# A lag-table generator with part of its arguments on ScalarE, its gate block interleaved, and its last output chunk in quarters

## The chip, the cores and the metric

One core of one Trainium2 chip. The metric is the device time of one execution in microseconds (us), median of the fast runs; a run more than 1.5% above the fastest of its kernel counts as slow and is left out. A profile is one execution; its span is about 1.7 us shorter than the time of the same execution. TensorE is called PE below, VectorE DVE, ScalarE ACT.

## The reference, cut to what matters

```python
x = A_u                                              # (1, 2048, 512)
g = sigmoid((x * gate_w).sum(-1, keepdims=True))     # the gate
a = ssm_conv(x)     # y = causal convolution of u with K, plus u*Dskip
b = moe(x)          # top 2 of 2048 tokens through one expert, scattered back onto x
return g * a + (1 - g) * b
# in ssm_conv:
P = exp(logdA[:, :, None] * l[None, None, :])        # complex, one row per lag l
K = einsum("dn,dnl,dn->dl", Cc, P, dB).real
```

The exponentials of all lags are built from two smaller tables: 32 coarse lags ("first table", groups of four, eight groups) and 21 fine lags ("second table", six groups, the last with one lag). The channels come in two halves, so each table is made twice.

## The kernel before

One group of four lags goes through these steps: `arg` (an angle in 16-bit turns, eight instructions), `sin` (one activation over the eight), `prod` (DVE multiplies with the decay that `exp` made on ACT; a *full product* below is the eight DVE instructions of a second-table group). `S.op` puts an instruction at the end of its engine's queue and derives its waits from the buffers it reads and writes; the program gives each engine one queue. A buffer is a name, not an address range: an instruction that writes `bYA[vb]` waits for everything that touched `bYA[vb]`, and also for the same engine's own earlier write to it.

```python
def lag_group(hh, lags, is_q, slot0, gi, stage):     # hh: half, is_q: second table, gi: buffer 0/1
    if stage == 'arg':
        for i, t in enumerate(lags):
            for cs in range(2):
                TS(ARG(...), B16(...), float(t), ALU.mult, [bB16], [bARG[gi]], s2=..., op1=ALU.add, eng=DVE)
    elif stage == 'exp':  ...   # one ACT instruction per lag
    elif stage == 'sin':
        ACTV(TRG(...gi...), ARG16(...gi...), ACTF.Sin, [bARG[gi]], [bTRG[gi]], ...)
    else: ...                   # prod: 2 DVE instructions (first table) or 8 (second table)
# ... [cut]
        def kgen_tables(hh):
            def block_(tab, is_q, ngr):
                lgp(0, 'arg'); lgp(1, 'arg')
                for g in range(ngr):
                    lgp(g, 'sin')
                    if not is_q and g == 5:
                        ...                       # the 21 exps of the second table
                    lgp(g, 'prod')
                    if g + 2 < ngr:
                        lgp(g + 2, 'arg')
                    if hh == 0: next(rm_gen, None)        # one step of routing and expert
                    else:       next(post_g[0], None)
            block_(LQ_T1, False, 8)
            block_(LQ_T2, True, 6)
            if hh == 0:
                ...                               # 32 exps of the second half's first table
```

Ahead of `kgen_tables(0)` stands the gate block: 64 transposes of the input on PE, eight evictions of them (copies of PE's results) on ACT into `XT`, four DVE multiplies, PE logits, sigmoid. After both tables of a half come 512 small strided matmuls (`kgen_mm`), then the spectral products. The last chunk's output is `xu_inv(3)`, `mix_a(3)`, `mix_p(3)`, `mix_o(3)`: eight evictions, one add, sixteen scalings on ACT, one add, one store, each over the whole chunk.

## Time and profile before

| | before |
|---|---|
| time, median of 16 runs | 394.99 us (392.92 to 397.87) |
| span of the profiled run | 396.1 us (that run: 397.87) |
| busy DVE / ACT / PE | 285.3 / 221.9 / 188.3 us |
| DVE busy in the gate block (24.2 to 43.6) | 5.5 of 19.4 us |

No engine is busy throughout. So what counts is not busy time but which wait ends last in each stage, and the working of the prediction reads it stage by stage from where one engine's instructions start. In a timeline row the columns are start, duration of the merged stretch, engine, line, operation, output and input with shapes, count, and in brackets the idle time just before and what ended it. L306 is the DVE helper with two tensor inputs, L309 a scaling, L310 the one that makes an argument, L314 a copy, L316 the activation helper; in the changed kernel L403 is an argument on ACT.

### The profile page before, as it was taken

To read this page: it belongs to the slowest core of one execution; us is meant where nothing else is said; L and a number is where in the kernel's file an instruction comes from. 1 tells how busy PE (TensorE), PEld (TensorE's weight loads), DVE (VectorE), ACT (ScalarE), POOL (GpSimd) and SP (SyncE) were. 2 spreads that over 40 slices of the span, in tenths; PEclk is the share of its full clock that TensorE was granted. 3 is DMA by queue.
4 is the path that set the end of the run, shared out by engine and by line. 5 is a ranking of instruction groups with operands and counts; after the bars stand their busy time and mean duration, and the time that the engine had idled before them with its cause. 6 is when DMAs were issued, how large, how long until landed. Compare 5 with 4: busy or idle time off the path is not lost.

```text
span 396.1 us, 8501 instructions
## 1 busy us (share of the span) xinstructions
PE 188.3 (48%) x3674; PEld 170.5 (43%) x3674; DVE 285.3 (72%) x537; ACT 221.9 (56%) x337; POOL 1.7 (0%) x6
## 2 busy tenths in 40 slices
PE   2503100331400073640179100779899999997900
PEld 2502000330100073530179100779879979885900
DVE  0842799525999995577149999999999099899331
ACT  3895453695313599768965225244553393571574
POOL 0000100000000000000000000000000000000000
PEclk9965555555855565585588855669978969968775
DMA  6998000031000000000000000000000000200222
GB/s 155 285 452 367 2 1 0 0 122 65 1 0 0 0 5 2 2 2 1 0 2 2 2 0 1 3 5 2 3 2 2 2 2 2 56 0 2 55 54 53
DMA packets 18213, 16.91 MB, mean 43 GB/s; under 512 B 12800, under 2 KB 17024, under 8 KB 18048
## 3 DMA queue, kind: packets, MB, share of 16 engines
q1 hardware_dynamic: 18176, 16.37, 12.5%
q8 instruction: 29, 0.48, 0.5%
q14 instruction: 8, 0.07, 0.1%
HBM read 14.27 MB, written 2.10 MB: 41 GB/s over the span
## 4 chain that ended last, share of the span: by engine, by line
DVE 37%; ACT 32%; PE 24%; issue 5%; SPq 1%; DMA 1%; ACTq 0%; DVEq 0%
DVE RT L306 23%; ACT RT L316 17%; DVE RT L310 11%; PE ps L729 9%; ACT RK L316 8%; PE ps L779 5%; ACT RT L793 3%; ACT L316 3%; PE ps L697 2%; PE ps L660 1%; PE ps L664 1%; PE ps L769 1%; PE ps L768 1%; ACT RS L316 1%; DMA RT<-in_A_C_im_dram 1%
## 5 line engine op out<-in xcount | busy, mean ns | idle before, releaser
L306 DVE TENSOR_TENSOR RT<-RT 128x1024 bf16<-128x1024 bf16 (+5 forms) x140 | 102.3, 743 | 34.8 <-ACT RT L316 17.6
L316 ACT ACTIVATE RT<-RT 128x2048 bf16<-128x2048 int16 (+1 forms) x28 | 50.9, 1817 | 59.3 <-DVE RT L310 59.3
L316 ACT ACTIVATE RT<-ps 128x512 bf16<-128x512 f32 (+3 forms) x79 | 52.3, 669 | 51.6 <-PE ps L729 22.8
L310 DVE TENSOR_SCALAR RT<-RS 128x256 int32<-128x256 f32 x212 | 70.3, 334 | 6.3
L306 DVE TENSOR_TENSOR RT<-RT,RK 128x4096 bf16<-128x4096 bf16 (+3 forms) x32 | 52.2, 1674 | 11.7 <-ACT RT L316 11.6
L660 PE MATMUL ps<-RT 128*32 128x24 bf16 x512 | 22.8, 290 | 65.0 <-DVE RT L306 65.0
L729 PE MATMUL ps<-RU,RC 128*128 128x128 bf16 x896 | 52.4, 222 | 2.6 <-ACT RK L316 2.6
L729 PEld LDWEIGHTS ps<-RU,RC 128*128 128x128 bf16 x896 | 51.8, 100 | 2.8 <-issue 2.8
L660 PEld LDWEIGHTS ps<-RT 128*32 128x32 bf16 x512 | 21.5, 173 | 66.3 <-DVE RT L306 65.3
L779 PE MATMUL ps<-RT,RC 128*128 128x128 bf16 x512 | 38.4, 252 | 3.0 <-DVE RT L306 3.0
L779 PEld LDWEIGHTS ps<-RT,RC 128*128 128x128 bf16 x512 | 37.7, 117 | 3.5 <-DVE RT L306 3.1
L697 PE MATMUL ps<-RS,RC 128*128 128x128 bf16 x288 | 21.5, 248 | 30.6 <-ACT RS L316 27.1
L697 PEld LDWEIGHTS ps<-RS,RC 128*128 128x128 bf16 x288 | 20.6, 114 | 31.4 <-ACT RS L316 27.6
L793 ACT ACTIVATE RT<-RT,RS 128x128 bf16<-128x128 bf16 x64 | 25.7, 401 | 14.2 <-DVE RT L306 12.2
L316 ACT ACTIVATE RT<-RS 128x256 bf16<-128x256 f32 x74 | 30.8, 416 | 3.5 <-DVE RS L306 1.2
L306 DVE TENSOR_TENSOR RT<-RK,RT 128x1024 bf16<-128x1024 bf16 x16 | 11.1, 691 | 26.5 <-ACT RT L316 26.3
L306 DVE TENSOR_TENSOR RT<-RT,RS 128x1024 bf16<-128x1024 bf16 (+1 forms) x48 | 27.7, 618 | 0.4
L316 ACT ACTIVATE RK<-ps 128x512 bf16<-128x512 f32 x32 | 19.1, 596 | 15.6 <-DVE RT L306 10.5
L664 PE MATMUL ps<-RT 128*32 128x24 bf16 x512 | 22.9, 290 | 4.2 <-issue 4.2
L664 PEld LDWEIGHTS ps<-RT 128*32 128x32 bf16 x512 | 21.9, 172 | 4.1 <-issue 4.1
L316 ACT ACTIVATE RK<-RS 128x256 bf16<-128x256 f32 x32 | 22.0, 687 | 1.0
L316 ACT ACT_TABLE_LOAD x12 | 15.4, 1283 | 0.9 <-PEq L869 0.7
(59 smaller groups left out, 149.6 us busy)
## 6 DMA issues: line engine op xcount, KB each, us to landing
RC<-c_mats SPq DMA_DIRECT2D x1, 5376.0 KB, 24.8
RU<-in_A_u_dram SPq DMA_DIRECT2D x4, 512.0 KB, 8.1
out_dram<-RT SPq DMA_DIRECT2D x4, 512.0 KB, 3.8
RK<-in_B_w_gate_dram SPq DMA_DIRECT2D x1, 1792.0 KB, 9.6
RK<-in_B_w_up_dram SPq DMA_DIRECT2D x1, 1792.0 KB, 13.7
RK<-in_B_w_down_dram SPq DMA_DIRECT2D x1, 1792.0 KB, 7.9
RT<-in_A_A_re_dram SPq DMA_DIRECT2D x1, 128.0 KB, 2.3
RT<-in_A_A_im_dram SPq DMA_DIRECT2D x1, 128.0 KB, 2.4
```

The lines of the kernel that those rows point to most:

```text
L306: return S.op(eng, lambda h: h.tensor_tensor(out=o, in0=a_, in1=b_, op=op), reads=rd, writes=wr)
L310: return S.op(eng, lambda h: h.tensor_scalar(out=o, in0=a_, scalar1=s1, scalar2=s2, op0=op0, op1=op1), reads=rd, writes=wr)
L316: return S.op(ACT, lambda h: h.activation(out=o, in_=a_, func=func, scale=scale), reads=rd, writes=wr)
L660: h.matmul(P32(b, 32 * c4, 32, cq * 24, (1, 24)), TP(0, 128, (ch // 8) * 512 + (ch % 8), (8, 32)), TQ(0, 128, ch, (HC, 24)), start=True, s ...
L664: last = h.matmul(P32(b, 32 * c4, 32, cq * 24, (1, 24)), TP(0, 128, (ch // 8) * 512 + 256 + (ch % 8), (8, 32)), TQ(0, 128, NSLOT * HC + ch ...
L697: last = h.matmul(P32(bb[hb_], 0, 128, tl * 128, (1, 128)), CM(0, 128, OF_KP + u * 1024 + tau * 128, (1, 128)), KC(0, 128, kb * 768 + KUSE ...
L729: last = h.matmul(P32(bb[hb_], 0, 128, tl * 128, (1, 128)), CM(0, 128, of + tc * 1024 + tau * 128, (1, 128)), U(0, 128, tb * D + ck * 128, ...
L768: h.matmul(P32(b, 0, 128, t_ * 128, (1, 128)), DG(0, 128, tb * 128, (1, 128)), U(0, 128, tb * D + ck * 128, (1, 128)), start=True, stop=False)
L769: last = h.matmul(P32(b, 0, 128, t_ * 128, (1, 128)), OHR(0, 2, tb * 128, (1, 128)), ZB(0, 2, ck * 128, (1, 128)), start=False, stop=True)
L779: last = h.matmul(P32(b, 0, 128, tt * 128, (1, 128)), CM(0, 128, OF_G + sc * 512 + tt * 128, (1, 128)), YHs[vb](0, 128, j * 1024 + sc * 12 ...
L793: S.op(ACT, lambda h, tb=tb, vb=vb: h.activation(out=YA(0, 128, vb * 2048 + tb * 128, (1, 128)), in_=YA(0, 128, vb * 2048 + tb * 128, (1, ...
```

## The change

Its title speaks of interleaving the gate computation into the lag generator and of pipelining the final chunk's output. It has four parts: (1) the gate block becomes the first steps of the generator that the first half draws from, two steps per group; (2) six of the eight arguments of each second-table group go to ACT; (3) in the second half the 21 exps move from group 5 to group 7; (4) the last chunk is finished in four quarters, scaled on DVE, each with its own store.

```diff
             if stage == 'arg':
...
+                        if is_q and (2 * i + cs) < 6:
+                            S.op(ACT, lambda h, ...: h.activation(out=ARG(...), in_=B16(...), func=ACTF.Copy,
+                                 scale=float(t), bias=(16384.0 if cs == 0 else 0.0)), reads=[bB16], writes=[bARG[gi]])
+                        else:
+                            TS(ARG(...), B16(...), float(t), ALU.mult, ..., eng=DVE)
...
         def routing_and_moe():
+            ...   # transposes, 8 evictions, multiplies, logits, sigmoid moved in here
+            yield ...
-                    if not is_q and g == 5:
+                    if not is_q and ((g == 7 and hh == 1) or (g == 5 and hh == 0)):
...
                     if hh == 0:
+                        next(rm_gen, None)
                         next(rm_gen, None)
...
+        def final_fine(ck):
+            ...   # four evictions of x as before, UD = u*Dskip
+            for j in range(NBLK):
+                ...   # 32 matmuls
+                ACTV(YA(quarter j), P32(b...), ACTF.Copy, [bps[b]], [bYA[vb]])
+                TT(YA, YA, UD, ALU.add, [bYA[vb], bUD[vb]], [bYA[vb]])
+                for t_ in range(4):
+                    TS(YA(128 columns), ..., SG(...), ALU.mult, [bYA[vb], bG32], [bYA[vb]])
+                TT(P2, P2, YA, ALU.add, [bP2[vb], bYA[vb]], [bP2[vb]])
+                S.dma(... out, quarter j ..., reads=[bP2[vb]], final=True)
...
-        xu_inv(3)
-        mix_a(3)
-        mix_p(3)
-        mix_o(3)
+        final_fine(3)
```

More of the change, by code (lines that the diff above doesn't have):

```diff
@@ L401, in lag_group @@
                     for cs in range(2):
-                        TS(ARG(0, 128, ((gi * 2 + cs) * 4 + i) * HC, (1, HC)), B16(0, 128, c0, (1, HC)), float(t), ALU.mult, [bB16], [bARG[gi]],
-                           s2=(16384.0 if cs == 0 else 0.0), op1=ALU.add, eng=DVE)
+                        if is_q and (2 * i + cs) < 6:
+                            S.op(ACT, lambda h, i=i, t=t, cs=cs: h.activation(out=ARG(0, 128, ((gi * 2 + cs) * 4 + i) * HC, (1, HC)), in_=B16(0, 128, c0, (1, HC)), func=ACTF.Copy,
+                                                                             scale=float(t), bias=(16384.0 if cs == 0 else 0.0)), reads=[bB16], writes=[bARG[gi]])
+                        else:
+                            TS(ARG(0, 128, ((gi * 2 + cs) * 4 + i) * HC, (1, HC)), B16(0, 128, c0, (1, HC)), float(t), ALU.mult, [bB16], [bARG[gi]],
+                               s2=(16384.0 if cs == 0 else 0.0), op1=ALU.add, eng=DVE)
             elif stage == 'exp':
@@ L444, in bass_gated_mix__ssm_conv_s4__moe_arch_mod__prompt_kernel @@
             lag_group(0, LQ_T1[4 * g_:4 * g_ + 4], False, 4 * g_, g_ % 2, 'exp')
-        for tb2 in range(NTB // 2):
-            b = bank()
-            def tr(h, tb2=tb2, b=b):
-                last = None
-                for t_ in range(2):
-                    for db in range(4):
-                        last = h.transpose(PBF(b, 0, 128, (t_ * 4 + db) * 128, (1, 128)),
-                                           U(0, 128, (2 * tb2 + t_) * D + db * 128, (1, 128)), IDENT(0, 128, 0, (1, 128)))
-                return last
-            S.op(PE, tr, reads=[bU[tb2 // 2], bID], writes=[bps[b]])
-            ACTV(XT(0, 128, tb2 * 256, (128, 2), (L, 4), (1, 128)), PBF(b, 0, 128, 0, (512, 2), (128, 4), (1, 128)), ACTF.Copy, [bps[b]], [bXT])
@@ L456, in bass_gated_mix__ssm_conv_s4__moe_arch_mod__prompt_kernel @@
-        bON = Buf("ones"); bWLF = Buf("wlf"); bLOG = Buf("log")
-        S.op(POOL, lambda h: h.memset(ONES(0, 128, 0, (1, 8)), 1.0), writes=[bON])
-        CP(WLF(0, 128, 0, (1, 8)), WLG(0, 128, 0, (1, 8)), [bWLG], [bWLF])
+        bOHT = Buf("oht"); bOHR = Buf("ohr"); bZ = Buf("z"); bRS = Buf("rs"); bZS = Buf("zs"); bDG = Buf("dg")
+        bON = Buf("ones"); bWLF = Buf("wlf"); bLOG = Buf("log"); bLP = Buf("logpart")
         bPTs = [Buf("pt0"), Buf("pt1")]
         bPT.parents.extend(bPTs)
-        b = bank()
@@ L462, in bass_gated_mix__ssm_conv_s4__moe_arch_mod__prompt_kernel @@
-        for db in range(4):
-            pb_ = db % 2
-            TS(PT(0, 128, pb_ * L, (1, L)), XT(0, 128, db * L, (1, L)), WLF(0, 128, db * 2, (1, 1)), ALU.mult, [bXT, bWLF], [bPTs[pb_]])
-            def lg(h, b=b, db=db, pb_=pb_):
-                last = None
-                for tb in range(NTB):
-                    h.matmul(P32(b, 0, 128, db * 32 + tb * 2, (1, 1)), PT(0, 128, pb_ * L + tb * 128, (1, 128)), ONES(0, 128, 0, (1, 1)), start=True, stop=True)
-                    last = h.matmul(P32(b, 0, 128, db * 32 + tb * 2 + 1, (1, 1)), XT(0, 128, db * L + tb * 128, (1, 128)), WLG(0, 128, db * 2 + 1, (1, 1)), start=True, stop=True)
-                return last
-            S.op(PE, lg, reads=[bXT, bPTs[pb_], bON, bWLG], writes=[bps[b]])
@@ L472, in bass_gated_mix__ssm_conv_s4__moe_arch_mod__prompt_kernel @@
-        bLP = Buf("logpart")
-        CP(RTS(0, 128, 64, (1, 128)), P32(b, 0, 128, 0, (1, 128)), [bps[b]], [bLP])
-        TT(LOG(0, 128, 0, (1, 32)), RTS(0, 128, 64, (1, 32)), RTS(0, 128, 96, (1, 32)), ALU.add, [bLP], [bLOG])
-        TT(LOG(0, 128, 0, (1, 32)), LOG(0, 128, 0, (1, 32)), RTS(0, 128, 128, (1, 32)), ALU.add, [bLP, bLOG], [bLOG])
-        TT(LOG(0, 128, 0, (1, 32)), LOG(0, 128, 0, (1, 32)), RTS(0, 128, 160, (1, 32)), ALU.add, [bLP, bLOG], [bLOG])
-        dbgout("logits", LOG(0, 128, 0, (1, 32)), [bLOG])
@@ L478, in bass_gated_mix__ssm_conv_s4__moe_arch_mod__prompt_kernel @@
-        bS = Buf("s"); bE = Buf("e"); bDEN = Buf("den"); bREC = Buf("rec"); bG = Buf("g"); bG32 = Buf("g32"); bOMG = Buf("omg"); bO32 = Buf("omg32"); bRB = Buf("rb")
-        CP(SGB(0, 128, 0, (1, 16)), LOG(0, 128, 0, (2, 16)), [bLOG], [bS])
-        CP(SGB(0, 128, 64, (1, 16)), LOG(0, 128, 1, (2, 16)), [bLOG], [bRB])
-        CP(SG(0, 128, 0, (1, 16)), SGB(0, 128, 64, (1, 16)), [bRB], [bRB])
-        ACTV(SGB(0, 128, 16, (1, 16)), SGB(0, 128, 0, (1, 16)), ACTF.Exp, [bS], [bE], scale=-1.0)
-        TS(SGB(0, 128, 32, (1, 16)), SGB(0, 128, 16, (1, 16)), 1.0, ALU.add, [bE], [bDEN])
@@ L484, in bass_gated_mix__ssm_conv_s4__moe_arch_mod__prompt_kernel @@
-        S.op(DVE, lambda h: h.reciprocal(out=SG(0, 128, 16, (1, 16)), in_=SGB(0, 128, 32, (1, 16))), reads=[bDEN], writes=[bREC])
-        CP(SGB(0, 128, 48, (1, 16)), SG(0, 128, 16, (1, 16)), [bREC], [bG])
-        CP(SG(0, 128, 32, (1, 16)), SGB(0, 128, 48, (1, 16)), [bG], [bG32])
-        TS(SGB(0, 128, 16, (1, 16)), SGB(0, 128, 48, (1, 16)), -1.0, ALU.mult, [bG], [bE, bOMG], s2=1.0, op1=ALU.add)
-        CP(SG(0, 128, 48, (1, 16)), SGB(0, 128, 16, (1, 16)), [bOMG], [bO32])
-        dbgout("g", SG(0, 128, 32, (1, 32)), [bG32, bO32])
@@ L491, in bass_gated_mix__ssm_conv_s4__moe_arch_mod__prompt_kernel, with tr, lg @@
-        bOHT = Buf("oht"); bOHR = Buf("ohr"); bZ = Buf("z"); bRS = Buf("rs"); bZS = Buf("zs"); bDG = Buf("dg")
-        def routing_and_moe():
+        bS = Buf("s"); bE = Buf("e"); bDEN = Buf("den"); bREC = Buf("rec"); bG = Buf("g"); bG32 = Buf("g32"); bOMG = Buf("omg"); bO32 = Buf("omg32"); bRB = Buf("rb")
+        def routing_and_moe():
+            for tb2 in range(NTB // 2):
+                b = bank()
+                def tr(h, tb2=tb2, b=b):
+                    last = None
+                    for t_ in range(2):
+                        for db in range(4):
+                            last = h.transpose(PBF(b, 0, 128, (t_ * 4 + db) * 128, (1, 128)),
+                                               U(0, 128, (2 * tb2 + t_) * D + db * 128, (1, 128)), IDENT(0, 128, 0, (1, 128)))
+                    return last
+                S.op(PE, tr, reads=[bU[tb2 // 2], bID], writes=[bps[b]])
+                ACTV(XT(0, 128, tb2 * 256, (128, 2), (L, 4), (1, 128)), PBF(b, 0, 128, 0, (512, 2), (128, 4), (1, 128)), ACTF.Copy, [bps[b]], [bXT])
+            yield
+            S.op(POOL, lambda h: h.memset(ONES(0, 128, 0, (1, 8)), 1.0), writes=[bON])
+            CP(WLF(0, 128, 0, (1, 8)), WLG(0, 128, 0, (1, 8)), [bWLG], [bWLF])
+            b = bank()
+            for db in range(4):
+                pb_ = db % 2
+                TS(PT(0, 128, pb_ * L, (1, L)), XT(0, 128, db * L, (1, L)), WLF(0, 128, db * 2, (1, 1)), ALU.mult, [bXT, bWLF], [bPTs[pb_]])
+                def lg(h, b=b, db=db, pb_=pb_):
+                    last = None
+                    for tb in range(NTB):
+                        h.matmul(P32(b, 0, 128, db * 32 + tb * 2, (1, 1)), PT(0, 128, pb_ * L + tb * 128, (1, 128)), ONES(0, 128, 0, (1, 1)), start=True, stop=True)
+                        last = h.matmul(P32(b, 0, 128, db * 32 + tb * 2 + 1, (1, 1)), XT(0, 128, db * L + tb * 128, (1, 128)), WLG(0, 128, db * 2 + 1, (1, 1)), start=True, stop=True)
+                    return last
+                S.op(PE, lg, reads=[bXT, bPTs[pb_], bON, bWLG], writes=[bps[b]])
+                if db % 2 == 1:
+                    yield
+            CP(RTS(0, 128, 64, (1, 128)), P32(b, 0, 128, 0, (1, 128)), [bps[b]], [bLP])
+            TT(LOG(0, 128, 0, (1, 32)), RTS(0, 128, 64, (1, 32)), RTS(0, 128, 96, (1, 32)), ALU.add, [bLP], [bLOG])
+            TT(LOG(0, 128, 0, (1, 32)), LOG(0, 128, 0, (1, 32)), RTS(0, 128, 128, (1, 32)), ALU.add, [bLP, bLOG], [bLOG])
+            TT(LOG(0, 128, 0, (1, 32)), LOG(0, 128, 0, (1, 32)), RTS(0, 128, 160, (1, 32)), ALU.add, [bLP, bLOG], [bLOG])
+            dbgout("logits", LOG(0, 128, 0, (1, 32)), [bLOG])
+            CP(SGB(0, 128, 0, (1, 16)), LOG(0, 128, 0, (2, 16)), [bLOG], [bS])
+            CP(SGB(0, 128, 64, (1, 16)), LOG(0, 128, 1, (2, 16)), [bLOG], [bRB])
+            CP(SG(0, 128, 0, (1, 16)), SGB(0, 128, 64, (1, 16)), [bRB], [bRB])
+            ACTV(SGB(0, 128, 16, (1, 16)), SGB(0, 128, 0, (1, 16)), ACTF.Exp, [bS], [bE], scale=-1.0)
+            yield
+            TS(SGB(0, 128, 32, (1, 16)), SGB(0, 128, 16, (1, 16)), 1.0, ALU.add, [bE], [bDEN])
+            S.op(DVE, lambda h: h.reciprocal(out=SG(0, 128, 16, (1, 16)), in_=SGB(0, 128, 32, (1, 16))), reads=[bDEN], writes=[bREC])
+            CP(SGB(0, 128, 48, (1, 16)), SG(0, 128, 16, (1, 16)), [bREC], [bG])
+            CP(SG(0, 128, 32, (1, 16)), SGB(0, 128, 48, (1, 16)), [bG], [bG32])
+            TS(SGB(0, 128, 16, (1, 16)), SGB(0, 128, 48, (1, 16)), -1.0, ALU.mult, [bG], [bE, bOMG], s2=1.0, op1=ALU.add)
+            CP(SG(0, 128, 48, (1, 16)), SGB(0, 128, 16, (1, 16)), [bOMG], [bO32])
+            dbgout("g", SG(0, 128, 32, (1, 32)), [bG32, bO32])
+            yield
@@ L785, in xu_inv, with xu, iv @@
                 S.dma(lambda h, ck=ck, vb=vb: [h.dma_start(dbg["yb"][ck, :, :], YA(0, 128, vb * 2048, (1, 2048)))], newsem(), reads=[bYA[vb]], final=True)
+        def final_fine(ck):
+            vb = ck % 2
+            for tq in range(4):
+                b = bank()
+                def xu(h, tq=tq, b=b, ck=ck):
+                    last = None
+                    for t_ in range(4):
+                        tb = 4 * tq + t_
+                        h.matmul(P32(b, 0, 128, t_ * 128, (1, 128)), DG(0, 128, tb * 128, (1, 128)), U(0, 128, tb * D + ck * 128, (1, 128)), start=True, stop=False)
+                        last = h.matmul(P32(b, 0, 128, t_ * 128, (1, 128)), OHR(0, 2, tb * 128, (1, 128)), ZB(0, 2, ck * 128, (1, 128)), start=False, stop=True)
+                    return last
+                S.op(PE, xu, reads=bU + [bDG, bOHR, bZS], writes=[bps[b]])
+                ACTV(P2(0, 128, vb * 2048 + tq * 512, (1, 512)), P32(b, 0, 128, 0, (1, 512)), ACTF.Copy, [bps[b]], [bP2[vb]])
+            TT(UD(0, 128, vb * 2048, (128, NTB), (1, 128)), U(0, 128, ck * 128, (D, NTB), (1, 128)), DSK(0, 128, ck * 128, (0, NTB), (1, 128)), ALU.mult, bU + [bDSK], [bUD[vb]])
+            for j in range(NBLK):
+                b = bank()
+                def iv(h, j=j, b=b, vb=vb):
+                    last = None
+                    for tt in range(4):
+                        for sc in range(8):
+                            last = h.matmul(P32(b, 0, 128, tt * 128, (1, 128)), CM(0, 128, OF_G + sc * 512 + tt * 128, (1, 128)),
+                                            YHs[vb](0, 128, j * 1024 + sc * 128, (1, 128)), start=(sc == 0), stop=(sc == 7))
+                    return last
+                S.op(PE, iv, reads=[bCM, bYH[vb]], writes=[bps[b]])
+                o = vb * 2048 + j * 512
+                ACTV(YA(0, 128, o, (1, 512)), P32(b, 0, 128, 0, (1, 512)), ACTF.Copy, [bps[b]], [bYA[vb]])
+                TT(YA(0, 128, o, (1, 512)), YA(0, 128, o, (1, 512)), UD(0, 128, o, (1, 512)), ALU.add, [bYA[vb], bUD[vb]], [bYA[vb]])
+                for t_ in range(4):
+                    tb = 4 * j + t_
+                    TS(YA(0, 128, o + t_ * 128, (1, 128)), YA(0, 128, o + t_ * 128, (1, 128)), SG(0, 128, 32 + tb, (1, 1)), ALU.mult, [bYA[vb], bG32], [bYA[vb]])
+                TT(P2(0, 128, o, (1, 512)), P2(0, 128, o, (1, 512)), YA(0, 128, o, (1, 512)), ALU.add, [bP2[vb], bYA[vb]], [bP2[vb]])
+                S.dma(lambda h, ck=ck, j=j, o=o: [h.dma_start(dr(out, 4 * j * 128 * D + ck * 128, (D, 128), (128 * D, 4), (1, 128)), P2(0, 128, o, (128, 4), (1, 128)))],
+                      newsem(), reads=[bP2[vb]], final=True)
```

## The prediction

> **What bounds the kernel now.** I read the page's engine totals and slices first, then the chain that ended last, then busy time by stretch, then the timelines of VectorE (DVE) and ScalarE (ACT) for starts.
>
> ```profile
> span 396.1 us, 8501 instructions
> PE 188.3 (48%) x3674; PEld 170.5 (43%) x3674; DVE 285.3 (72%) x537; ACT 221.9 (56%) x337; POOL 1.7 (0%) x6
> DVE  0842799525999995577149999999999099899331
> ACT  3895453695313599768965225244553393571574
> DVE 37%; ACT 32%; PE 24%; issue 5%; SPq 1%; DMA 1%; ACTq 0%; DVEq 0%
> ```
>
> No engine bounds the whole run: in the first 60% of the slices DVE and ACT take turns at 9, and the chain is 37% DVE and 32% ACT, two engines handing work to each other. Busy time by stretch (us, then instructions per engine):
>
> ```profile
> 24.20:43.60 19.40, 3.97 (x128) 3.75 (x128) 5.51 (x19) 11.68 (x16) 1.38 (x1) 0.50 0.76 324
> 43.60:72.70 29.10, 2.12 (x7) 0.94 (x8) 26.72 (x89) 11.07 (x7) 0.00 (x0) 0.50 0.00 1
> 102.70:140.20 37.50, 0.35 (x15) 0.25 (x10) 36.03 (x80) 14.51 (x18) 0.00 (x0) 0.57 0.00 0
> 211.20:247.30 36.10, 8.40 (x151) 8.23 (x148) 34.69 (x76) 14.64 (x17) 0.00 (x0) 0.68 0.00 0
> 370.30:396.10 25.80, 5.74 (x97) 5.56 (x94) 4.81 (x4) 17.39 (x40) 0.00 (x0) 0.70 0.22 49
> ```
>
> 24.2 to 43.6 is the gate block: DVE busy 5.51 of 19.4 us. The three middle rows are parts of the lag generator, DVE nearly full. The last row is the final chunk, ACT and DVE in turn. The timeline rows whose durations I use:
>
> ```profile
> 12.39 14.30 ACT L316 ACTIVATE RT<-RS 128x256 bf16<-128x256 f32 x32 [1.22 <-DVE RS L306]
> 26.60 8.82 ACT L316 ACTIVATE RT<-ps 128x1024 bf16<-128x1024 bf16 x8
> 35.45 1.42 DVE L309 TENSOR_SCALAR RT<-RT,RS 128x2048 bf16<-128x2048 bf16 x2 [11.14 <-ACT RT L316]
> 49.96 2.59 DVE L310 TENSOR_SCALAR RT<-RS 128x256 int32<-128x256 f32 x8
> 90.14 1.42 DVE L306 TENSOR_TENSOR RT<-RT 128x1024 bf16<-128x1024 bf16 x2 [7.91 <-ACT RT L316]
> 97.79 4.88 PE L598 MATMUL ps<-RK,RS 128*2 128x512 bf16 x14 [12.33 <-DVE RS L306]
> 370.32 6.91 ACT L793 ACTIVATE RT<-RT,RS 128x128 bf16<-128x128 bf16 x16 [10.95 <-DVE RT L306]
> 383.63 6.90 ACT L793 ACTIVATE RT<-RT,RS 128x128 bf16<-128x128 bf16 x16 [1.29 <-DVE RT L306]
> ```
>
> Third row: DVE waits 11.14 us for the transposed input, which ACT evicts behind 32 exps. Fifth: DVE waits 7.91 us while ACT runs 21 exps. Sixth: the expert's down projection, 4.88 us, is hidden today behind 16 argument instructions. Strides from start to start: eight arguments 2.50 us, one exp 0.447, one sine 1.91, a two-multiply product 1.33, a full eight-multiply product of the second table 5.19 (102.66 to 107.85).
>
> **What the Trainium skill says.** "ScalarE: Activation LUTs", § What ACT_TABLE_LOAD costs, gives 1283 ns for a load plus about 1380 ns of drain. The trace has 1.28 us and the sine starting 0.02 us later (73.00, then 74.30): I use 1.28. The same section gives 186 ns + 0.833 ns per element for immediate scale and bias: 399 ns at 256 elements, against 416 measured for the exp, so an argument moved to ACT should cost like an exp. § Rules for kernel authors there says to put multiplies on VectorE; the trace agrees on price (0.31 on DVE, 0.45 in series on ACT), but ACT has the spare time. "Perfetto Trace Analysis", § Optimization Strategy, says regimes with different bounds may gain from interleaving; that is the intent here. Whether they gain depends on what each insertion waits for.
>
> **The change, part by part.** I walk the changed order of instructions with the strides above, to about 0.05 us per hand-over.
>
> *1. Gate block inside the first table (first half).* DVE issues 16 arguments at 24.2 (to 29.2). ACT ends its exps at 26.7, loads the sine table, ends sine 0 at 29.9, so product 0 starts at 29.9 instead of 48.6: 18.7 us early. But ACT then runs all eight transposes' evictions (8.8, to 38.7), because the first step of the generator issues them all, and they are one buffer, so DVE's logit multiply waits until 38.7 and sine 1 too. Product 1 starts at 40.7 (was 53.1). Two more multiplies end at 45.9; PE's two batches of logits put the DVE copy at 47.5; the sum and casts let the gate's exp run at 49.0; with two table loads (one before, one after) sine 2 ends at 52.45. Product 2: 52.5 (was 57.9). Product 3: 58.0 (was 63.0). Then two routing rounds per group, the second waiting about 0.65 us for a PE transpose: product 4 at 64.75 (was 67.8). The routing exp with its two loads: product 5 at 74.8 (was 76.2). The 21 exps, 9.4 us on ACT: product 6 at 88.9 (was 90.1). Then the expert: DVE finishes the hidden values at 91.3, the down projection runs until 96.2, and the copy of its result stands in DVE's order before product 7. Product 7 therefore starts at 97.2 (was 95.2), the rest of the routing ends at 99.0, the four remaining DVE arguments and sine follow, and the first product of the second table starts at 101.6 (was 102.66). Of 18.7 us won at the start, **1.05 us** is left: the interleaved work creates waits in DVE's in-order queue that the old placement hid.
>
> *2. Arguments of the second table on ACT.* Six of eight per group move. DVE per group: 8 x 0.3125 = 2.50 falls to 0.62, saving 1.88; the last group's two (0.6) move too. ACT per group: 6 x 0.447 + 1.91 = 4.6, below DVE's new 5.19 + 0.62 = 5.81, so hidden in the first half. Saving 3 x 1.88 + 0.55 = 6.2, plus about 1.35 of routing work (0.97 and 0.44) no longer in this stretch: **7.5 us**. First half ends at 131.7 instead of 140.2: **8.55 us** with part 1. The following stage (140.2 to 161.1: 32 exps beside PE's strided matmuls) starts its exps after the last sine as before and just shifts.
>
> *3. Second half.* Sine 5 ends at 185.4 in old time. Moving the 21 exps behind sine 7 lets products 5 to 7 run without them: sine 7 ends at 193.8. Then ACT does a load 1.28, exps 9.38, two evictions 1.2, twelve arguments 5.37, a load 1.28, sine 1.91: product q0 at 214.25. Before, 211.20. So the placement loses **3.05 us**: twelve arguments that DVE did in an idle stretch now lie in series on ACT. Then 5.81 per group again, ACT now 4.6 + 1.2 of evictions = 5.8, just level; four groups and two short tails end at 244.3, plus 0.2 for near ties: 244.5 instead of 247.3. Net **2.8 us**.
>
> *4. Final chunk in quarters.* Before: eight evictions, an add (1.24), sixteen scalings on ACT (6.9), an add (1.23), then a 512 KB store (3.8). After: eviction j 0.65, add 0.45, four DVE scalings at 0.287 = 1.15 (stride of the sixteen 128x128 tensor-scalar instructions at 277.7), add 0.45. First quarter's last add ends at about 382.45. The quarters don't overlap: one buffer for the result makes eviction j+1 wait for the add of j, and the output buffer makes the add of j+1 wait for the store of j. A 128 KB store should take about 2.4 (128 KB parameter loads with the same 256-byte pieces: 2.3 to 2.8). Period 0.45 + 2.5 = 2.95; last add ends at 391.3 (before 391.8), store 2.4 and close 0.5: 394.2 to 394.5. Gain **1.6 us**; the pipeline is worth only the smaller last store.
>
> Sum: 8.55 + 2.8 + 1.6 = 12.95 us; 396.35 - 12.95 = **383.4 us**, 3.3% faster. Parts 1 and 4, the named ones, give 2.7; the arguments give the rest.
>
> **The rivals.** *A: the gate block vanishes whole.* DVE was busy only 5.5 of 19.4 us there, so 13 us more could go: about 371. For it: product 0 starts 18.7 us early. Against: ACT's exps and table loads and PE's down projection stay in series; it would need ACT to reach the 21 exps much earlier, which the routing chain forbids. *B: ACT becomes the bound.* 32 arguments per half, each 0.45 and each waiting for the one before (same buffer); if the conversion to integer were slower on ACT, say 0.6, q groups in the second half would take about 6.7 and the twelve arguments 1.8 more, costing some 5 us: about 388. The trace shows no conversion to integers on ACT, so this stays open. *C: the stores serialize the tail.* If a small store took 3.5 us, four in series would make the tail 2.5 us longer than before: 387.5. *D: the later PE-bound stage (granted clock 0.81 to 0.92) is granted less because load comes earlier:* a few us either way.
>
> **Range and chances.** The largest doubts are part 1 (a stall of 2 to 3 us either way, as when the down-projection weights land at about 90.5, only 0.8 before they are needed), rival B (5 us) and C (4 us). I put 8 chances in 10 on 379.0 to 388.5. 2% is 388.4: faster 0.86, same 0.12, slower 0.02.
>
> **What would show it.** Right: in DVE's timeline the first product near 30 us, a wait of about 5 us for the evictions up to 38.7, a wait of about 5 us for PE's down projection before the eighth product; first q product near 101.6; first half's table end near 132; a wait of DVE of nearly 19 us behind exps and arguments before the second half's first q product (old time 195 to 214); in the tail, four stores each followed by the next add. ACT arguments at 0.42 each. Wrong: ACT arguments over 0.5, DVE waits for ACT inside the q groups, or a first q product earlier than 97, which would mean that the order does hide more than I give it.

## The result, and the profile after

376.29 us, median of 11 runs (374.22 to 377.57), against 394.99; ratio 0.9523, interval 0.9497 to 0.9549. A ratio here is the mean time of one kernel's fast runs over that of the other's of the same rounds, so not quite the ratio of the two medians. The gain is 18.8 us (395 x 0.0477). The forecast was 13 us and the range ended at 379.0: right direction, too small by 5.9 us, outside the range. The prediction counts from 396.35 us, a figure that no run has; from 394.99 its forecast would be 382.0 and the lower end of its range 377.6, still above the result.

Busy time by stretch, with the boundaries set where the same work starts in both kernels. The columns are the stretch and its length, then busy us and instruction count of PE, PE weight loads, DVE, ACT and GpSimd, the granted clock, the DMA share and GB/s. Before:

```profile
24.20:102.66 78.46, 17.52 (x344) 12.56 (x345) 46.14 (x152) 45.98 (x54) 1.38 (x1) 0.51 0.26 104
102.66:140.20 37.54, 0.39 (x17) 0.29 (x12) 36.07 (x80) 14.51 (x18) 0.00 (x0) 0.57 0.00 0
140.20:163.02 22.82, 13.33 (x608) 12.71 (x608) 13.08 (x17) 21.98 (x28) 0.00 (x0) 0.57 0.02 4
163.02:211.20 48.18, 19.90 (x317) 19.51 (x318) 28.99 (x80) 35.27 (x48) 0.00 (x0) 0.65 0.01 1
211.20:247.30 36.10, 8.40 (x151) 8.23 (x148) 34.69 (x76) 14.64 (x17) 0.00 (x0) 0.68 0.00 0
247.30:344.40 97.10, 91.64 (x1846) 85.21 (x1846) 83.52 (x88) 45.66 (x81) 0.00 (x0) 0.86 0.03 8
344.40:396.10 51.70, 28.63 (x316) 23.92 (x315) 30.17 (x29) 28.23 (x64) 0.00 (x0) 0.72 0.14 32
```

After:

```profile
24.42:102.27 77.85, 18.47 (x354) 12.95 (x354) 44.43 (x143) 50.36 (x66) 1.38 (x1) 0.52 0.25 98
102.27:132.10 29.83, 0.00 (x0) 0.00 (x0) 29.04 (x55) 25.70 (x46) 0.00 (x0) 0.50 0.00 0
132.10:150.96 18.86, 13.07 (x608) 12.44 (x608) 12.70 (x18) 18.27 (x20) 0.00 (x0) 0.59 0.02 4
150.96:202.27 51.31, 22.06 (x336) 21.50 (x336) 25.64 (x69) 39.35 (x60) 0.00 (x0) 0.67 0.01 1
202.27:232.00 29.73, 8.95 (x128) 8.66 (x128) 28.94 (x54) 23.11 (x37) 0.00 (x0) 0.67 0.00 1
232.00:325.96 93.96, 88.88 (x1846) 82.97 (x1846) 82.93 (x88) 44.66 (x81) 0.00 (x0) 0.91 0.03 7
325.96:374.70 48.74, 28.31 (x316) 23.45 (x315) 35.20 (x51) 21.81 (x48) 0.00 (x0) 0.73 0.16 35
```

Row by row, before minus after: 0.6 (everything up to the first full product of the second table), 7.7 (that table, first half), **4.0** (the 32 exps beside the strided matmuls), -3.1 (first table, second half), 6.4 (second table, second half), 3.1 (spectral products), 3.0 (last products and final chunk). The first, second, fourth and fifth answer to the walk (1.05, 7.5, -3.05, 5.85). The third was forecast as zero, the last as 1.6. The sixth holds the same code in both; the granted clock differs (0.86, 0.91), and `e12` below shows how far that stretch varies by itself. The rows add up to 21.6 us, more than the 18.8 of the timed runs: the profiled run of the kernel before was the slowest of its sixteen.

The first half's DVE timeline after the change: the first product, the multiply that waits for the evictions, the copy that waits for the down projection, and the first full product.

```profile
30.21 1.42 DVE L306 TENSOR_TENSOR RT<-RT 128x1024 bf16<-128x1024 bf16 x2 [0.70 <-ACT RT L316]
...
38.94 1.42 DVE L309 TENSOR_SCALAR RT<-RT,RS 128x2048 bf16<-128x2048 bf16 x2 [4.73 <-ACT RT L316]
...
96.95 0.68 DVE L314 CAST RS<-ps 2x512 bf16<-2x512 f32 x1 [5.51 <-PE ps L607]
...
102.27 1.29 DVE L306 TENSOR_TENSOR RT<-RT 128x1024 bf16<-128x1024 bf16 x2 [1.45 <-ACT RT L316]
```

Both announced waits are there (4.73 and 5.51 us), and the 18 us won at 30 are gone at 102.

Now the stage that was forecast as a mere shift. ACT's timeline before, from the fourth sine of the second table to the 32 exps:

```profile
127.24 1.91 ACT L316 ACTIVATE RT<-RT 128x2048 bf16<-128x2048 int16 x1 [6.21 <-DVE RT L310]
132.95 0.63 ACT L316 ACTIVATE RT<-RT 128x512 bf16<-128x512 int16 x1 [3.81 <-DVE RT L310]
133.60 1.28 ACT L316 ACT_TABLE_LOAD   x1
134.89 22.95 ACT L316 ACTIVATE RK<-RS 128x256 bf16<-128x256 f32 x32
```

After (the exps' row merges all 32):

```profile
115.78 0.86 ACT L403 ACTIVATE RT<-RS 128x256 int32<-128x256 f32 x2
119.55 2.43 ACT L316 ACTIVATE RT<-RT 128x2048 bf16<-128x2048 int16 x2 [2.90 <-DVE RT L310]
122.00 1.28 ACT L316 ACT_TABLE_LOAD   x1
123.29 22.49 ACT L316 ACTIVATE RK<-RS 128x256 bf16<-128x256 f32 x32
```

Before, the last sine (0.63 us) waits 3.81 us for DVE: its two arguments stand in DVE's queue behind the fourth full product. After, ACT has made them itself (0.86 us at 115.78) and the last sine runs right behind the one before. The exps start 11.6 us earlier while the table ends only 8.1 us earlier: a head start of 3.5 us over the strided matmuls, and in both of these traces the critical chain of the stage that follows runs through ACT's exps.

The final chunk before, DVE's timeline (the last two adds):

```profile
382.37 1.23 DVE L306 TENSOR_TENSOR RT<-RT 128x2048 bf16<-128x2048 bf16 x1 [2.75 <-ACT RT L316]
390.56 1.23 DVE L306 TENSOR_TENSOR RT<-RT 128x2048 bf16<-128x2048 bf16 x1 [6.97 <-ACT RT L793]
```

After, DVE's timeline, then ACT's:

```profile
361.86 0.42 DVE L306 TENSOR_TENSOR RT<-RT 128x512 bf16<-128x512 bf16 x1 [0.68 <-ACT RT L316]
362.32 1.12 DVE L309 TENSOR_SCALAR RT<-RT,RS 128x128 bf16<-128x128 bf16 x4
363.48 0.42 DVE L306 TENSOR_TENSOR RT<-RT 128x512 bf16<-128x512 bf16 x1
364.63 0.42 DVE L306 TENSOR_TENSOR RT<-RT 128x512 bf16<-128x512 bf16 x1 [0.72 <-ACT RT L316]
365.09 1.12 DVE L309 TENSOR_SCALAR RT<-RT,RS 128x128 bf16<-128x128 bf16 x4
366.25 0.42 DVE L306 TENSOR_TENSOR RT<-RT 128x512 bf16<-128x512 bf16 x1
```

```profile
364.00 0.60 ACT L316 ACTIVATE RT<-ps 128x512 bf16<-128x512 f32 x1 [2.17 <-DVE RT L306]
366.77 0.60 ACT L316 ACTIVATE RT<-ps 128x512 bf16<-128x512 f32 x1 [2.17 <-DVE RT L306]
```

A quarter takes 364.63 - 361.86 = 2.77 us, a ring of DVE and ACT: the next eviction waits 2.17 us for the add, then DVE waits 0.72 for the eviction. The second quarter's last add (366.25) follows its scalings without a pause, so it did not wait for the first store, which the page gives 2.0 us from issue to landing (3.8 for a whole chunk).

### The profile page after: what moved, and what is told of

The parts are those of the page before. It is cut to its first block, busy times and chain, and to the rows that moved or that the text cites. A ratio compares the mean times of both kernels' runs of the same rounds, so it can differ in the third digit from the quotient of the medians.

```text
span 374.7 us, 8503 instructions
## 1 busy us (share of the span) xinstructions
PE 187.9 (50%) x3674; PEld 169.5 (45%) x3674; DVE 271.4 (72%) x495; ACT 238.9 (64%) x385; POOL 1.7 (0%) x6
## 4 chain that ended last, share of the span: by engine, by line
ACT 36%; DVE 32%; PE 25%; issue 4%; DMA 1%; SPq 1%; ACTq 0%; DVEq 0%
DVE RT L306 23%; ACT RT L316 20%; PE ps L739 10%; ACT RK L316 8%; DVE RT L310 5%; PE ps L789 5%; ACT L316 3%; PE ps L707 2%; ACT RT L837 2%; PE ps L674 1%; PE ps L670 1%; PE ps L607 1%; PE ps L779 1%; PE ps L778 1%; DVE RT L309 1%
## 5 line engine op out<-in xcount | busy, mean ns | idle before, releaser
L306 DVE TENSOR_TENSOR RT<-RT 128x1024 bf16<-128x1024 bf16 (+5 forms) x146 | 103.8, 722 | 29.7 <-ACT RT L316 19.3
L316 ACT ACTIVATE RT<-ps 128x512 bf16<-128x512 f32 (+3 forms) x79 | 51.8, 662 | 55.9 <-PE ps L739 22.8
L310 DVE TENSOR_SCALAR RT<-RS 128x256 int32<-128x256 f32 x148 | 51.2, 348 | 19.1 <-ACT RT L403 14.9
L739 PE MATMUL ps<-RU,RC 128*128 128x128 bf16 x896 | 55.0, 227 | 17.7 <-ACT RK L316 17.7
L739 PEld LDWEIGHTS ps<-RU,RC 128*128 128x128 bf16 x896 | 54.1, 102 | 18.1 <-issue 17.6
L306 DVE TENSOR_TENSOR RT<-RT,RK 128x4096 bf16<-128x4096 bf16 (+3 forms) x32 | 51.1, 1641 | 9.2 <-ACT RT L316 9.1
L670 PE MATMUL ps<-RT 128*32 128x24 bf16 x512 | 22.3, 284 | 52.1 <-DVE RT L306 52.1
L707 PEld LDWEIGHTS ps<-RS,RC 128*128 128x128 bf16 x288 | 20.9, 115 | 21.0 <-ACT RS L316 17.2
L403 ACT ACTIVATE RT<-RS 128x256 int32<-128x256 f32 x64 | 26.4, 416 | 1.9
L837 ACT ACTIVATE RT<-RT,RS 128x128 bf16<-128x128 bf16 x48 | 19.2, 401 | 12.5 <-DVE RT L306 11.1
L789 PE MATMUL ps<-RT,RC 128*128 128x128 bf16 x384 | 26.6, 242 | 0.0
L789 PEld LDWEIGHTS ps<-RT,RC 128*128 128x128 bf16 x384 | 26.1, 111 | 0.3
L674 PE MATMUL ps<-RT 128*32 128x24 bf16 x512 | 22.5, 283 | 4.5 <-issue 4.5
```

Of the source, the lines that this page charges most:

```text
L306: return S.op(eng, lambda h: h.tensor_tensor(out=o, in0=a_, in1=b_, op=op), reads=rd, writes=wr)
L310: return S.op(eng, lambda h: h.tensor_scalar(out=o, in0=a_, scalar1=s1, scalar2=s2, op0=op0, op1=op1), reads=rd, writes=wr)
L316: return S.op(ACT, lambda h: h.activation(out=o, in_=a_, func=func, scale=scale), reads=rd, writes=wr)
L403: S.op(ACT, lambda h, i=i, t=t, cs=cs: h.activation(out=ARG(0, 128, ((gi * 2 + cs) * 4 + i) * HC, (1, HC)), in_=B16(0, 128, c0, (1, HC)), ...
L670: h.matmul(P32(b, 32 * c4, 32, cq * 24, (1, 24)), TP(0, 128, (ch // 8) * 512 + (ch % 8), (8, 32)), TQ(0, 128, ch, (HC, 24)), start=True, s ...
L674: last = h.matmul(P32(b, 32 * c4, 32, cq * 24, (1, 24)), TP(0, 128, (ch // 8) * 512 + 256 + (ch % 8), (8, 32)), TQ(0, 128, NSLOT * HC + ch ...
```

## The experiments

Every kernel was correct. The batches ran on different chips, so gains are taken from ratios to the kernel before of the same rounds, times 395; the changed kernel itself stands at 0.9523. The theory for the missing 5.9 us: 4 of it are the head start of the 32 exps, 1.4 the tail. The rival: that stage just shifts, and what the traces differ by there is contention or clock.

**Two instructions alone** (`e1`), on the kernel before:

```diff
+                        if is_q and ng == 1 and hh == 0:     # last group, first half: ACT
```

> The kernel before, with only two instructions moved: the two arguments of the last, one-lag group of the second table, first half, from VectorE to ScalarE. Head-start theory: they no longer stand behind the fourth full product in VectorE's queue, so the last sine of that half can run right behind the sine before it (about 129.2 instead of 132.95 us), the 32 exps that follow start near 131.1 instead of 134.9, and since ScalarE alone bounds the stage after, the second half's first product comes 3.8 us earlier: gain 3.5 to 4.2 us, near 391.2 against 395. Rival (my walk on record: that stage just shifts, and what the changed kernel won there is contention or clock): only the two arguments' own 0.6 us, near 394.4.

388.85 us, ratio 0.9846 (0.9818 to 0.9875): gain 6.1 us. Its ACT timeline:

```profile
120.94 0.86 ACT L403 ACTIVATE RT<-RS 128x256 int32<-128x256 f32 x2
127.12 2.43 ACT L316 ACTIVATE RT<-RT 128x2048 bf16<-128x2048 int16 x2 [5.31 <-DVE RT L310]
129.56 1.28 ACT L316 ACT_TABLE_LOAD   x1
130.86 20.06 ACT L316 ACTIVATE RK<-RS 128x256 bf16<-128x256 f32 x32
```

The exps start 4.0 us earlier (130.9; 131.1 was expected), and the second half's first product 5.5 us earlier (157.50 against 163.02). The rival's 0.6 us is excluded. The gain is larger than the 3.5 to 4.2 expected, because these 32 exps also took 20.06 instead of 22.95 us, of which PE, now last to finish, gave back about 1.4. An excess of that size is within what this stage varies by without any edit to it (below).

**The two instructions put back** (`e2`), on the changed kernel:

```diff
-                        if is_q and (2 * i + cs) < 6:
+                        if is_q and (2 * i + cs) < 6 and not (ng == 1 and hh == 0):
```

> The changed kernel with only those two instructions put back on VectorE. Head-start theory: the 32 exps start near 127.2 instead of 123.3 us and the second half's first product comes at about 154.9 instead of 151.0: 3.9 us slower, near 380.1. Rival (stage just shifts): 0.6 us slower, near 376.9.

380.75 us, ratio 0.9633 (0.9604 to 0.9663): 4.3 us slower than the changed kernel (0.0110 x 395).

```profile
126.69 0.63 ACT L316 ACTIVATE RT<-RT 128x512 bf16<-128x512 int16 x1 [3.81 <-DVE RT L310]
127.34 1.28 ACT L316 ACT_TABLE_LOAD   x1
128.64 20.65 ACT L316 ACTIVATE RK<-RS 128x256 bf16<-128x256 f32 x32
```

The wait of 3.81 us is back, word for word as before. The exps start 5.35 us later than in the changed kernel (123.29); 1.44 of that stood there already at the first full product (103.71 against 102.27), so 3.9 belong to the edit, as expected. Taken from both sides, two instructions of 0.3 us are worth 4.3 to 6.1 us.

**The gate block alone** (`e3`), on the kernel before: only part 1.

```diff
         def routing_and_moe():
+            ...   # gate block moved in;  arguments, exps and final chunk as before
```

> The kernel before with only the gate block interleaved into the lag generator; arguments on VectorE, exps and final chunk as before. My walk: first product near 30 us, but the first product of the second table near 104 (16 arguments on VectorE after the expert's result at 99), 1.4 us later than before; 1.4 us of routing leaves the stretch behind it: gain 0, within 1 us of 395. Rival (the interleaving named in the change's title is what pays): 5 us or more.

394.89 us, ratio 0.9991 (0.9957 to 1.0024): gain 0.4 us, not told from zero. Its first full product starts at 104.93, where 104 was expected. The part that the title names first pays nothing that can be told alone.

**The final chunk alone** (`e4`), on the kernel before:

```diff
-        xu_inv(3); mix_a(3); mix_p(3); mix_o(3)
+        final_fine(3)
```

> The kernel before with only the final chunk in quarters. From the changed kernel's trace (22.8 us from the last mix to the end, 25.8 before): gain 3.0 us, near 392. What is on record (each quarter waits for the store before it): gain 1.6 us, near 393.4.

392.47 us, ratio 0.9927 (0.9882 to 0.9971): gain 2.9 us. The interval reaches from 1.1 to 4.7 and so holds 1.6 too; the trace, with the same 2.77 us per quarter and 22.8 us instead of 25.8 from the start of the third chunk's scalings on ACT to the end, decides for 3.0.

**The arguments alone** (`e5`), on the kernel before: only part 2, both halves.

```diff
+                        if is_q and (2 * i + cs) < 6:     # ACT, nothing else changed
```

> The kernel before with only the second table's arguments on ScalarE (both halves). Sum of terms: first half 6.2 us from VectorE's shorter groups and 4.0 from the head start of the 32 exps, second half 2.3 (36.1 to 30.0 per table, less 3.8 for twelve arguments in series before its first product): gain 12.5 us, near 382.5. If the head start were not there (the walk on record): gain 8.5, near 386.5.

380.61 us, ratio 0.9621 (0.9580 to 0.9661): gain 15.0 us, more than the 12.5 of the sum. In its trace both tables of both halves are done at 232.02, the changed kernel's at 232.03: up to there part 2 alone has as much gain as all parts. In that trace the stage of the 32 exps gave 5.4 us where 4.0 were expected (the exps took 19.83 us, before 22.95), the first table of the first half 0.6 where nothing was, and the second half's loss was 3.4 instead of 3.8: most of the excess over 12.5, and the first of the three may be chance.

**The second half's exps back at group 5** (`e6`), on the changed kernel:

```diff
-                    if not is_q and ((g == 7 and hh == 1) or (g == 5 and hh == 0)):
+                    if not is_q and g == 5:
```

> The changed kernel with the second half's 21 exps back behind its sixth sine, nothing else. My walk: the first product of the second table, second half, would come 0.65 us later (the last two sines then each wait for a product and two evictions after the exps): 0.5 to 1 us slower, near 377. Rival (the move is what shortened the second half): 3 us or more slower.

377.45 us, ratio 0.9541 (0.9498 to 0.9583): 0.7 us slower, as expected, though the intervals overlap. Part 3 is worth less than the timed runs can tell; in the traces the way from the second half's first product to its first full product takes 51.86 us against 51.31.

Within their noise the four parts add: 0.4 + 15.0 + 0.7 + 2.9 = 19.0 against 18.8 measured together.

**Quarters tracked one by one** (`e7`), on the changed kernel's final chunk, same memory and instructions:

```diff
+            bP2q = [Buf('p2q%d' % q, parents=[bP2[vb]]) for q in range(4)]
+            bYAq = [Buf('yaq%d' % q, parents=[bYA[vb]]) for q in range(4)]
...   # every bYA[vb] of quarter j becomes bYAq[j], every bP2[vb] becomes bP2q[j]
```

> The changed kernel with the final chunk's result and output tracked per quarter instead of per chunk (same memory, same instructions, fewer waits). If the one-buffer wait sets the tail (each eviction waits for the add of the quarter before, 2.77 us per quarter in the trace), the quarter falls to VectorE's own 2.08: 3 x 0.69 = 2.1 us faster, near 374.2. If the store or the matmuls set it, no change.

373.25 us, ratio 0.9449 (0.9415 to 0.9482): 2.9 us faster than the changed kernel, 2.1 expected. DVE now runs without a pause:

```profile
360.90 1.12 DVE L309 TENSOR_SCALAR RT<-RT,RS 128x128 bf16<-128x128 bf16 x4
362.06 0.76 DVE L306 TENSOR_TENSOR RT<-RT 128x512 bf16<-128x512 bf16 x2
362.86 1.12 DVE L309 TENSOR_SCALAR RT<-RT,RS 128x128 bf16<-128x128 bf16 x4
364.01 0.76 DVE L306 TENSOR_TENSOR RT<-RT 128x512 bf16<-128x512 bf16 x2
```

A quarter takes 362.86 - 360.90 = 1.96 us instead of 2.77, and the first quarter's wait for ACT (0.68 at 361.86 in the changed kernel) is gone too, which the expected 2.1 left out. This edit takes away both the eviction's wait and the store's wait; that the store's was idle is read from the trace above, not from this run.

**Routing's last steps later** (`e8`), on the changed kernel:

```diff
-                        next(rm_gen, None)
-                        next(rm_gen, None)
+                        for _n in range(1 if is_q else (2 if g < 6 else (1 if g == 6 else 0))):
+                            next(rm_gen, None)
```

> The changed kernel with the last steps of routing drawn later: the copy of the down projection's result stands behind the first full product of the second table in VectorE's queue, not before the first table's last product. If the 5.5 us that VectorE waits for that projection are on the path, the first product of the second table comes at 97.8 instead of 102.3 us: 4.4 us faster, near 371.9. If they only hide another wait (ScalarE's twelve arguments end at 95.8), less than 1 us.

373.93 us (371.63 to 376.30), ratio 0.9458 (0.9418 to 0.9498): 2.6 us faster, between the two expectations. The first full product in its trace:

```profile
97.28 1.29 DVE L306 TENSOR_TENSOR RT<-RT 128x1024 bf16<-128x1024 bf16 x2 [1.18 <-ACT RT L316]
```

97.8 was expected, and 102.27 is the changed kernel's. Of these 5.0 us 3.6 are left at the end of the first half's table (128.5 against 132.1), because routing's last steps, 1.4 us, now stand inside it; the expected 4.4 left that out. The timed runs scatter too widely to tell 2.6 from 3.6. So the 5.5 us of waiting for the down projection are on the path: work moved into a queue created them.

**The gate block put back** (`e9`), on the changed kernel: parts 2, 3 and 4 without part 1.

```diff
         def routing_and_moe():
-            ...   # gate block out again, ahead of the tables
```

> The changed kernel with only the gate block put back ahead of the lag generator; arguments on ScalarE, later exps and quartered final chunk stay. If the interleaving is worth nothing also beside the other parts (alone 0.3 us; with the arguments alone the tables end at 232.0 us, where the changed kernel's end): within 1.5 us of the changed kernel's 376.3. Rival (it pays only together with ScalarE's arguments): 3 us or more slower.

376.90 us, ratio 0.9556 (0.9508 to 0.9604): 1.3 us slower with an interval that reaches over zero. The tables end at 231.72, the changed kernel's at 232.03. But the exps' stage, which varies by chance, lies in between (17.8 us here, 18.8 in the changed kernel). Before it, the first full product comes at 101.84 here and at 102.04 in `e5`, no later than with the gate block inside (102.27). The table after it then takes 31.3 us in both, against 29.8, because routing's last steps are still in it. So in the traces part 1 is worth 1.0 us at the end of the first half's table (133.1 against 132.1); in the timed runs it is not shown to be worth anything, and more than about 3.5 us is excluded.

**Two groups' arguments back on DVE in the second half** (`e10`), on the changed kernel:

```diff
-                        if is_q and (2 * i + cs) < 6:
+                        if is_q and (2 * i + cs) < 6 and not (hh == 1 and slot0 < 8):
```

> The changed kernel with the arguments of the second half's first two groups back on VectorE, which idles there for 13 us behind ScalarE's 21 exps. If the twelve ScalarE arguments lie in series on the path (my walk), the first product of the second table comes 5.2 us earlier (197.1 instead of 202.3): near 371.1. If they only fill a wait for something else: no change.

370.39 us, median of five fast runs (370.68 with the slow one), ratio 0.9379 (0.9324 to 0.9434): 5.7 us faster, 5.2 expected. Its profiled run counts as slow (373.95, over 1.5% above the fastest, 367.03) and is left out of the ratio; only the order within it is read here:

```profile
184.87 5.08 DVE L310 TENSOR_SCALAR RT<-RS 128x256 int32<-128x256 f32 x16
198.62 1.29 DVE L306 TENSOR_TENSOR RT<-RT 128x1024 bf16<-128x1024 bf16 x2 [8.66 <-ACT RT L316]
```

The sixteen arguments fill DVE's idle time behind ACT's 21 exps; from the second half's first product to this one it is 46.2 us (152.39 to 198.62), 51.3 in the changed kernel.

**All three repairs** (`e11`): `e7`, `e8` and `e10` together.

> The changed kernel with all three repairs: routing's last steps drawn later (2.6 measured, 4.8 in its trace), quarters tracked one by one (2.9), two groups' arguments back on VectorE (5.2 expected). If they add: 10.7 to 12.9 us faster, 363.5 to 365.5. If ScalarE takes over as the bound between them: less than 9.

366.26 us (364.01 to 367.35), ratio 0.9273 (0.9227 to 0.9319): 28.7 us faster than the kernel before and 9.9 faster than the changed one, a little short of the 10.7 to 12.9 that adding gives, within the noise of its parts. It beats both kernels.

**The kernel before once more** (`e12`), for a second trace:

> The kernel before, unchanged, for a second trace. Two questions. The stretch from the first spectral product to the last one's start took 97.1 us in its first trace and 93.5 to 96.0 in others whose code there is the same: if that is spread, it should fall anywhere in 93 to 97.5 again. And the 32 exps beside the strided matmuls took 22.95 us in its first trace, 19.8 to 22.5 in others: if that belongs to the program, it is within 0.3 of 22.95 again; if it is chance from run to run, it moves by more than 1.

The stretch of spectral products took 95.4 us, the 32 exps 23.81. The first is inside the spread of all fourteen traces (93.4 to 97.1, same code in all), so the 3.1 us of the sixth row above are not shown to be a gain of the change. The spread goes with the granted clock: in the six traces at 0.89 or more the stretch took 93.4 to 93.9 us, in the eight at 0.88 or less 95.1 to 97.1, and `e3`, which leaves nearly everything as before, is among the six (0.91, 93.55). What sets the clock was not tried. The second moved by 0.86, between its two expectations, so this run does not decide. Other traces do: the changed kernel, `e6` and `e7` have the same instructions up to that point, and their 32 exps took 22.49, 22.49 and 19.57 us (`e10`, the slow run, 23.43). So they vary by chance by about 3 us, and the stage from the end of the table to the second half's first product by 1.7 (18.8, 18.8, 17.2).

The head start can still be told from that chance, by all traces of fast runs together. In four (the kernel before, `e2`, `e3`, `e4`) the exps start 5.3 us before the table ends, and the stage took 20.5 to 22.8 us, mean 21.9. In eight (the changed kernel, `e1`, `e5` to `e9`, `e11`) they start 8.8 us before, and it took 17.2 to 18.8, mean 17.9. The groups don't overlap, and their means differ by 4.0. (The two traces left out, `e10`'s slow run and `e12`'s single run of unknown state, took 19.8 with the head start and 23.7 without.)

## Why the prediction was wrong, point by point

- **Gate block, 1.05 us left of 18.7: the stalls held, the booking did not.** Both stalls were at the place and of the size announced, and the first full product came 0.6 us earlier. But `e5` and `e9` reach it as early with the gate block outside, so those 0.6 us are not the gate block's: with the arguments on ACT, what it brings is the routing that leaves the next table. That the total came out near is partly luck. Rival A is gone.
- **Second-table arguments, 7.5 us: held.** Traces 7.7, of which 6.3 are the arguments (`e5`: 37.5 to 31.3 us; 6.2 forecast) and the rest routing. The ACT arguments cost 416 ns each, like an exp, so rival B, a slow conversion to integers, did not occur.
- **"The following stage ... starts its exps after the last sine as before and just shifts": this step failed.** Zero was forecast; 4.0 us came in the trace, 4.3 to 6.1 in the two runs that move only those two instructions. The walk asked only what moving arguments saves DVE. It booked the last group's two (0.6 us) as work and not as a release: they let the last sine, and with it ACT's next long job, run before DVE's fourth product ends. In the changed kernel the last sine runs at 121.4, while that product ends at 124.6; only the product's first two multiplies read the buffer that the sine overwrites, so it was free.
- **Second half, 2.8 us: held.** Traces 6.4 - 3.1 = 3.3; the loss of 3.05 before its first full product was measured as 3.1, and `e10` wins it back.
- **Final chunk, 1.6 us: the mechanism half right, the term too small.** The one-buffer wait sets the quarter, as said (2.77 us against 2.95), which `e7` bears out: without it, and without the store's wait, a quarter takes 1.96. In the trace the wait for the store never came last: a 128 KB store took 2.0 us, not 2.4. Gain 2.9 to 3.0. Of the missing 1.4, 0.6 are the quarters (last add at 390.7 on the old time scale, not 391.3), 0.4 the store, and 0.3 its own rounding (391.3 + 2.4 + 0.5 = 394.2, which is a gain of 1.9). Rival C is gone.
- **Rival D** (another grant of the clock): the PE-bound stretch did go with the granted clock, but it varies by 3.7 us with the same code, and no trace shows the change as the cause.
- **The range.** It left 4.4 us on the fast side (383.4 to 379.0), argued mainly from part 1's stalls; a term of zero that could be 4 was not among its doubts. The sum of terms with their measured sizes is 0.6 + 7.7 + 4.0 + 3.3 + 3.0 = 18.6.

What stays open: why the 32 exps beside the strided matmuls cost anywhere from 19.6 to 23.8 us, and whether a head start also shortens them: their mean is 22.0 us in the four traces without it and 20.9 in the eight with it, less than they vary by chance.

## What to carry to other kernels

When an instruction moves from one engine's in-order queue to another, count not its duration but what it stood behind: the smallest group here, two instructions of 0.3 us, freed a job of some 20 us on the other engine 3.5 us sooner. Follow that for every buffer to the last instruction that really reads it. And interleaving a stalled block moves its waits into another queue rather than removing them, so look for the wait that now stands ahead of unrelated work, and draw it later.

## What the Trainium skill lacked or had wrong

- "ScalarE: Activation LUTs", § What ACT_TABLE_LOAD costs: a switch of tables costs 2.66 us there, with the drain. In these traces it cost 1.28 us: a sine started at 74.30 after a load at 73.00 (the activation ahead of the load had ended at 72.99), and in the changed kernel exps at 123.29 after a load at 122.00.
- The same page has no price for an ACT instruction that writes 32-bit integers from fp32. Measured: 416 ns for 128x256 (64 of them), the same as an exp to bf16 of that size; its formula gives 399.
- "SBUF — State Buffer", § SBUF: two separate sides, says that PE, ACT and DVE's dedicated pair of ports never wait on anyone. 32 exps of 128x256 took 14.3 us with no strided matmuls beside them (12.39 to 26.69) and 19.6 to 23.8 where they run beside them in part, and sixteen DVE arguments took 13.63 instead of 5.08. After those matmuls, from 153.40 in the kernel before, ten exps took 4.44 us, the usual 0.44 each. Whether the ports are the cause was not tried; something slows both engines there.
- No page that bears on this has the cost of a buffer tracked as one name though used in parts. Here it was 0.8 us per quarter (2.77 against 1.96).
